# A banded-attention and two-MoE kernel on one core: keys of batch 0 read once, other DMA costs in the planner, and an order picked by a search

## The chip, the cores and the metric

One NeuronCore of a Trainium2 chip runs the whole program. The metric is the device time in microseconds (us) of one execution; the time shown is the median of three. The engines that matter are PE (TensorE: matrix products), DVE (VectorE), ACT (ScalarE), POOL (GpSimd) and SP, whose queue issues every DMA of this kernel. Each engine runs its own instructions strictly in the order in which they were written for it, and waits on semaphores for the others.

## The reference

```python
B, H, S, D = 4, 8, 576, 64            # q, k, v in float32
q_d, k_d, v_d = mean over groups of 4 positions
out_d = softmax(q_d k_d^T / 8) v_d    # "global": 144 x 144 per head
out_up = repeat(out_d, 4)
# "local": keys within 3 positions of the query
scores = where(|i - j| < 4, q k^T / 8, -1e9)
x = out_up + softmax(scores) v        # -> 2304 tokens x 512
h = x @ w_in                          # 512 -> 1024
e = exp(h - max(h)); solu = h * e / (sum(e) + 1e-9)
x = (layernorm(solu) * g_ln) @ w_out  # 1024 -> 512
h = x @ w2_in                         # 512 -> 2048
out = (h * cos(h)) @ w2_out           # 2048 -> 512
```

The four weight matrices arrive in float64. The kernel reads each word pair as integers and builds the float32 value with three DVE operations (`wload`).

## The kernel before, in words

Every product of the two MoE layers is written as three float32r products of a high and a low part (`split` makes the two parts with one ACT and one DVE operation, `mm3` issues the three matmuls). The 2304 tokens go through the first MoE layer in nine groups of 256 (`xsplit`, `h1_half`, `h1_ln`, `ln_t`, `x2`), while the attention is still running; the second layer follows with one plain group of 256 and four groups of 512 by a Strassen-like scheme (`plain_h`, `plain_o`, `quad_h`, `quad_o`).

Attention is made of two kinds of items. A `Glob` (batch b, pair of heads c) does the downsampled attention: `load_qk` reads the whole q and k of two pairs at once (tiles `qt`, `kt`), `load` reads the v of one pair (tile `gv`, 72 partitions), `prep` pools q and k over four positions (DVE, L539) and v (L541, L543), then S, T and V are scores and softmax, transposes, and the product with v. A `Loc` (batch b, third t of the sequence, head group) does the banded attention of 192 queries: its `load` reads a window of q into the block-diagonal tile `diag` (two DMAs on 64 partitions, L594), a window of k (tile `kw`, L596) and windows of v (tile `lv`, L600); S is a mask product on identity weights plus the scores (L606, L608), and V adds the global result and writes `X` (L632). The windows that a `Loc` reads of q and k are the same numbers that `load_qk` reads for the globals.

`X` holds the 2304 tokens (36 blocks of 64). Its still unused tail serves as staging for weights (`stage`, `stage_early`, `stage_dead`, L422 for the load, L427, L429, L431 for the three DVE operations).

The text order of the program is not the order that runs. `arrange` takes all recorded instructions, builds their dependences (`connect`), and list-schedules them: each instruction has an estimated duration (`Step.estimate`), `deadlines` gives it a due time, `forwards` plays the engines and always takes the ready instruction that is due first, `backwards` does the same from the end and gives new due times. Of 2 times 20 plays the order with the earliest estimated end is kept and forced on every engine. A DMA is priced as start + bytes / rate + end, with at most eight in flight. 100 matmuls on the identity (`idle`, L735) need nothing but the mask and are due never, so that they stand on PE wherever the play found nothing else ready; their bank is needed again before the second use of the tag `m`.

Of the kernel before, what the change touches and what calls it, by code (L numbers as in the profile page):

```python
# [1 line left out]

# [18 lines left out]
QB = 64  # L21
# [13 lines left out]
ROUNDS = 20  # L35

# [11 lines left out]
DMA_ISSUE, DMA_START, DMA_END, DMA_RATE, DMA_FLIGHT = 475.0, 1100.0, 935.0, 250.0, 8  # L48
# [50 lines left out]
class Step:  # L99
# [102 lines left out]

def arrange(tc, pools, reopened):
# [9 lines left out]
    def pick(queue, free, ready, rank, last=None):  # L213

        t0, e = min((max(free.get(e, 0.0), min(ready[s] for s in q)), e) for e, q in queue.items() if q)
        q = queue[e]
        s = min((s for s in q if ready[s] <= t0), key=rank)
        if last and e == "PE" and s.mode != last.mode:
            like = [x for x in q if ready[x] <= t0 and x.mode == last.mode and not x.idle]
            if like:  # L220
                x = min(like, key=rank)
                if rank(x)[0] <= rank(s)[0] + PATIENCE:
                    s = x
        q.remove(s)
        return e, s, t0

    def forwards(due, switch):
        left = {s: len(s.preds) for s in steps}
        ready = dict.fromkeys(steps, 0.0)
        queue, free, order, start = {}, {}, {}, {}  # L230
        ticks, last, bus, flying, end = {}, None, 0.0, [], 0.0
        for s in steps:
            if not left[s]:
                queue.setdefault(s.engine, []).append(s)
        for _ in steps:
            e, s, t = pick(queue, free, ready, lambda s: (due[s], s.at), last)
            more = 0.0
            if s.dma:
# [3 lines left out]
                flying.append(bus + DMA_END)  # L242
                more = bus + DMA_END - t - s.ns
                free[e] = t + DMA_ISSUE
            else:
                if e == "PE":
                    t += switch if last and last.mode != s.mode else 0.0
                    last = s
                    if ticks.get(int(t / CLOCK_TICK) - 1, 0.0) < CLOCK_COLUMNS:
                        more = s.ns  # L250
                    i = int((t + s.ns + more) / CLOCK_TICK)
                    ticks[i] = ticks.get(i, 0.0) + s.count
                free[e] = t + s.ns + more
            start[s] = t
            end = max(end, t + s.ns + more)
            order.setdefault(e, []).append(s)
            for b in s.succs:
                ready[b] = max(ready[b], t if b.preds[s] == "begin" else t + after(s, b) + more)
                left[b] -= 1
                if not left[b]:  # L260
                    queue.setdefault(b.engine, []).append(b)
        return start, end, order

    def backwards(start):

        hold = {s: max(DMA_ISSUE, s.bytes / DMA_RATE) if s.dma else s.ns for s in steps}
        late = {s: -(start[s] + s.ns) for s in steps}
        left = {s: len(s.succs) for s in steps}
        ready = dict.fromkeys(steps, 0.0)
        queue, free, begin = {}, {}, {}  # L270
        for s in steps:
            if not left[s]:
                queue.setdefault(s.engine, []).append(s)
        for _ in steps:
            e, s, t = pick(queue, free, ready, lambda s: (-NEVER if s.idle else late[s], -s.at))
            begin[s] = -(t + hold[s])
            free[e] = t + hold[s]
            for a in s.preds:
                ready[a] = max(ready[a], t + hold[s] + after(a, s) - hold[a])
                left[a] -= 1  # L280
                if not left[a]:
                    queue.setdefault(a.engine, []).append(a)
# [818 lines left out]
```

## Time and profile before

| | |
|---|---|
| median of 3 runs | 770.74 us (765.24 to 772.59) |
| the profiled execution, its own time | 774.4 us |
| its span from first to last instruction | 772.6 us |
| busy in it | PE 750.3, DVE 619.1, ACT 448.9, POOL 18.8 us |
| DMA | 106.04 MB, 137 GB/s on the mean |

How to read it: the terms of the prediction are made against the span and the own time of that one execution, 1.8 us apart, and only then carried to the median. A view of windows gives the busy time of each engine in a stretch, so that stretch minus busy is its idle time; PEclk is the granted share of TensorE's clock and "DMA share" the mean busy share of the core's 16 DMA engines. In a timeline, brackets behind a row give the idle time ahead of it and what ended it.

### The profile page before, as it was taken

The page shows a single profiled execution, that of the slowest core. Times are in us where ns is not written, and L with a number is a line of the kernel's source. Part 1 is how long each engine was busy: PE and PEld are TensorE (multiplying, and loading weights), DVE is VectorE, ACT ScalarE, POOL GpSimd, SP SyncE. Part 2 cuts the span into 40 slices and gives each one's busy share as a digit, 9 for nine tenths or more (in the row PEclk, how much of TensorE's full clock was granted, in tenths as well). Part 3 has the DMA queues.
Part 4 walks back from the last instruction along what each step waited for, and adds up shares of the span by engine and source line. Part 5 has one row for each costly group of instructions (what it writes and reads, how often), then busy time and mean ns, then how long its engine had stood idle before and what let it go on. Part 6 is the DMA issues. An engine that isn't in the chain of part 4 may idle for free.

```text
span 772.6 us, 14725 instructions
## 1 busy us (share of the span) xinstructions
PE 750.3 (97%) x5444; PEld 647.4 (84%) x5444; DVE 619.1 (80%) x1379; ACT 448.9 (58%) x1036; POOL 18.8 (2%) x38
## 2 busy tenths in 40 slices
PE   5899999999999999999999999999999999999997
PEld 3566788897888887989988988988898889889896
DVE  5799999999988789776289998777778676887673
ACT  2466776756646455445377766565556665556544
POOL 3000000000000000000000000000000000000000
PEclk9799999999999999999999999999999999999999
DMA  9987865767785657631356433223211331113211
GB/s 237 260 237 197 239 165 176 192 175 223 217 265 145 201 165 229 210 108 39 107 150 178 137 120 99 56 82 110 69 43 54 123 97 44 39 56 108 56 29 54
DMA packets 86520, 106.04 MB, mean 137 GB/s; under 512 B 26384, under 2 KB 59440, under 8 KB 86448
## 3 DMA queue, kind: packets, MB, share of 16 engines
q1 hardware_dynamic: 86448, 105.10, 46.7%
q8 instruction: 43, 0.70, 0.4%
q14 instruction: 29, 0.24, 0.1%
HBM read 87.77 MB, written 17.30 MB: 136 GB/s over the span
## 4 chain that ended last, share of the span: by engine, by line
PE 54%; DVE 29%; DMA 8%; issue 4%; ACT 3%; POOL 1%; SPq 1%; DVEq 0%; POOLq 0%; ACTq 0%
PE s L399 6%; PE s L398 6%; PE s L397 6%; PE oa L397 4%; PE oa L399 3%; PE oa L398 3%; PE ob L397 3%; PE ob L398 3%; PE ob L399 3%; DMA X<-in_w2i_dram 3%; DVE P L390 3%; PE x L398 2%; DVE e L675 2%; DVE sm L491 2%; PE x L399 2%
## 5 line engine op out<-in xcount | busy, mean ns | idle before, releaser
L397 PE MATMUL x<-P,R 128*128 128x256 f32 x288 | 81.2, 284 | 1.5 <-ACT P L389 1.5
L398 PE MATMUL x<-P,R 128*128 128x256 f32 x288 | 81.3, 283 | 0.2 <-DVE P L390 0.2
L399 PE MATMUL x<-P,R 128*128 128x256 f32 x288 | 81.2, 283 | 0.0
L399 PE MATMUL s<-R,S_l 128*128 128x256 f32 x256 | 71.8, 282 | 0.0
L398 PE MATMUL s<-R 128*128 128x256 f32 x256 | 71.5, 280 | 0.0
L397 PE MATMUL s<-R 128*128 128x256 f32 x256 | 71.0, 281 | 0.0
L397 PE MATMUL h<-R,P 128*128 128x512 f32 x144 | 61.1, 424 | 0.5 <-DVE e L675 0.4
L494 ACT ACTIVATE le<-ls,sm 128x70 f32<-128x70 f32 x144 | 44.3, 320 | 26.3 <-DVE sm L492 12.8
L398 PE MATMUL h<-R,P 128*128 128x512 f32 x144 | 58.8, 408 | 0.0
L399 PE MATMUL h<-R,P 128*128 128x512 f32 x144 | 58.5, 406 | 0.0
L397 PEld LDWEIGHTS x<-P,R 128*128 128x128 f32 x288 | 54.0, 188 | 2.8 <-ACT P L389 2.3
L398 PEld LDWEIGHTS x<-P,R 128*128 128x128 f32 x288 | 54.2, 188 | 1.4 <-DVE P L390 1.1
L399 PEld LDWEIGHTS x<-P,R 128*128 128x128 f32 x288 | 54.2, 188 | 1.0 <-issue 0.8
L398 PE MATMUL s<-R,w2i 128*128 128x256 f32 x192 | 54.2, 283 | 0.2 <-DVE R L390 0.2
L399 PE MATMUL s<-R,w2i 128*128 128x256 f32 x192 | 54.0, 282 | 0.0
L397 PE MATMUL s<-R,w2i 128*128 128x256 f32 x192 | 53.8, 282 | 0.0
L389 ACT ACTIVATE GR<-a 128x1024 fp32r<-128x1024 f32 (+1 forms) x40 | 39.1, 977 | 24.3 <-DVE a L895 24.3
L389 ACT ACTIVATE w2i<-wo 128x512 fp32r<-128x512 f32 x58 | 36.2, 624 | 23.5 <-PE ob L399 15.8
L398 PEld LDWEIGHTS s<-R 128*128 128x128 f32 x256 | 48.3, 189 | 0.7
L399 PEld LDWEIGHTS s<-R,S_l 128*128 128x128 f32 x256 | 48.4, 189 | 0.0
L397 PEld LDWEIGHTS s<-R 128*128 128x128 f32 x256 | 47.8, 188 | 0.8
L892 ACT ACTIVATE a<-a 128x1024 f32<-128x1024 f32 (+1 forms) x40 | 38.9, 972 | 15.6 <-DVE a L890 15.5
(164 smaller groups left out, 2195.3 us busy)
## 6 DMA issues: line engine op xcount, KB each, us to landing
wo<-drw SPq DMA_DIRECT2D x80, 256.0 KB
X<-in_w2o_dram SPq DMA_DIRECT2D x32, 256.0 KB
X<-in_w2i_dram SPq DMA_DIRECT2D x32, 256.0 KB
lv<-in_vl_dram SPq DMA_DIRECT2D x48, 105.0 KB
kt<-in_k_dram SPq DMA_DIRECT2D x8, 594.0 KB
kw<-in_k_dram SPq DMA_DIRECT2D x24, 198.0 KB
qt<-in_q_dram SPq DMA_DIRECT2D x8, 576.0 KB
diag<-in_q_dram SPq DMA_DIRECT2D x48, 96.0 KB
```

Of the source, the lines that this page charges most:

```text
L389: nc.scalar.activation(out=hi, in_=src, func=AF.Copy)
L390: nc.vector.tensor_tensor(out=lo, in0=src, in1=hi.bitcast(F32), op=ALU.subtract)
L397: nc.tensor.matmul(ps, lh, rh, start=start, stop=False)
L398: nc.tensor.matmul(ps, lh, rl, start=False, stop=False)
L399: nc.tensor.matmul(ps, ll, rh, start=False, stop=stop)
L491: nc.vector.tensor_reduce(out=neg, in_=src, axis=AX.X, op=ALU.max, negate=True)
L494: nc.scalar.activation(out=e[:, j, :], in_=src[:, j, :], func=AF.Exp, bias=neg[:, j:j + 1], scale=scale, accum_out=ssum[:, j:j + 1])
L675: nc.vector.scalar_tensor_tensor(out=s, in0=p, scalar=GAIN, in1=s, op0=ALU.mult, op1=ALU.mult, accum_out=st[:, 2 + i:3 + i])
L892: nc.scalar.activation(out=a, in_=a, func=AF.Sin, scale=0.5)
```

## The change

Four things are changed.

1. For batch 0, `kt` no longer lies in the `qk` buffers but in `X` (ten of the blocks from block 9 on, which batch 1 fills later). A `Loc` of batch 0 takes its keys from there instead of reading `kw` again (6 loads fewer). For the first two thirds of batch 0 the block-diagonal `diag` is filled by ACT from `qt` (8 copies) instead of by DMA (8 loads fewer). Both `load_qk` of batch 0 stand first in the text.
2. `gv` is read in two DMAs of 64 and 8 partitions instead of one of 72 (16 loads more).
3. The planner's DMA price: the rate is 235 instead of 250 bytes per ns, bytes count 1.5 times where the contiguous run is under 512 bytes, and a DMA on fewer than 128 partitions with over 128 columns lands 2,000 ns later.
4. After the 40 plays, 78 fixed random draws are applied to the best due times, each shifting the due times of some (tile, engine) groups within some stretch of time; the result is played once and kept if its estimated end is earlier. `forwards`, `backwards` and `deadlines` are rewritten with heaps and lists over instruction numbers; apart from `land` and `bytes` they price what they did.

```diff
-DMA_ISSUE, DMA_START, DMA_END, DMA_RATE, DMA_FLIGHT = 475.0, 1100.0, 935.0, 250.0, 8
+DMA_ISSUE, DMA_START, DMA_END, DMA_RATE, DMA_FLIGHT = 475.0, 1100.0, 935.0, 235.0, 8
+DMA_RUN, DMA_SHORT, DMA_PART = 512, 1.5, 2000.0
+SEARCHED = 1.0
+DRAWS = (80000010, 80000013, 80000019, 80000027, 80000037, 80000077, 80000279, 80000333, 80000445, 80000518,
...
@@ Step.estimate
         if self.dma:
             self.bytes = n * list(out.ap)[0][1] * width(out)
-            return DMA_START + self.bytes / DMA_RATE + DMA_END
+            if list(out.ap)[-1][1] * width(out) < DMA_RUN:
+                self.bytes *= DMA_SHORT
+            self.land = DMA_END + (DMA_PART if list(out.ap)[0][1] < 128 and n > 128 else 0.0)
+            return DMA_START + self.bytes / DMA_RATE + self.land
...
+def draws(seed):
+    s = (seed * 2862933555777941757 + 3037000493) % 2 ** 62
+    for i in range(4):
+        s = (s * 6364136223846793005 + 1442695040888963407) % 2 ** 62
+    while True:
+        s = (s * 6364136223846793005 + 1442695040888963407) % 2 ** 62
+        yield s >> 31
...
@@ arrange, behind the 40 plays
+    names = [s.outs[0].bass_ap.tensor.name + s.engine for s in steps]
+    rank = {g: i for i, g in enumerate(sorted(set(names)))}
+    known = [d for d in chosen if abs(d) < NEVER / 2]
+    lo, hi = min(known), max(known)
+    due = chosen
+    for seed in DRAWS:
+        r = draws(seed)
+        at = lo + (hi - lo) * SEARCHED * (next(r) % 100000 / 100000.0)
+        wide = (10e3, 30e3, 100e3, 300e3, 2 * (hi - lo))[next(r) % 5]
+        size = (100.0, 300.0, 1000.0, 3000.0, 6000.0)[next(r) % 5]
+        share = (3, 10, 30, 100)[next(r) % 4]
+        shift = []
+        for _ in rank:
+            u = next(r) % 100
+            x = (next(r) % 2001 - 1000) / 500.0 * size
+            shift.append(x if u < share else 0.0)
+        due = [d + shift[rank[g]] if at - wide / 2 <= d < at + wide / 2 else d for d, g in zip(due, names)]
+    start, end, order = forwards(due, MODE_SWITCH)
+    if end < best:
+        best, kept, chosen = end, order, due
...
@@ Glob.load_qk
-                QK[self.b, self.c // 2] = [att.tile([128, NT3, 2, QT + 2 * HALO], F32, tag="qk", name=n, bufs=3)[:, :, :, :w]
-                                           for n, w in (("qt", QT), ("kt", QT + 2 * HALO))]
+                d = QK[self.b, self.c // 2] = []
+                for n, w in (("qt", QT), ("kt", QT + 2 * HALO)):
+                    if self.b == 0 and n == "kt":
+                        x = X[:, S // QB + 5 * (self.c // 2):][:, :5].rearrange("p b k q -> p (b k q)")
+                        d.append(x[:, :NT3 * 2 * w].rearrange("p (t h s) -> p t h s", t=NT3, h=2))
+                    else:
+                        d.append(att.tile([128, NT3, 2, QT + 2 * HALO], F32, tag="qk", name=n, bufs=3)[:, :, :, :w])
@@ Glob.load
-            nc.sync.dma_start(out=self.v, in_=vg[self.b, self.c])
+            for r in (slice(0, 64), slice(64, SH)):
+                nc.sync.dma_start(out=self.v[r], in_=vg[self.b, self.c, r])
@@ Loc.load
-                kt = att.tile([128, 2, QT + 2 * HALO], F32, tag="k", name="kw", bufs=2)
                 for j in range(2):
                     r = slice(64 * j, 64 * j + 64)
-                    nc.sync.dma_start(out=diag[i][r, :, :, j, :],
-                                      in_=q[self.b, self.cc, r, self.t].rearrange("p h (a s) -> p h a s", a=NB))
-                nc.sync.dma_start(out=kt, in_=k[self.b, self.cc, :, self.t])
+                    if self.b == 0 and self.t < 2:
+                        nc.scalar.copy(out=diag[i][r, :, :, j, :],
+                                       in_=QK[0, self.cc][0][r, self.t].rearrange("p h (a s) -> p h a s", a=NB))
+                    else:
+                        nc.sync.dma_start(out=diag[i][r, :, :, j, :],
+                                          in_=q[self.b, self.cc, r, self.t].rearrange("p h (a s) -> p h a s", a=NB))
+                if self.b == 0:
+                    kt = QK[0, self.cc][1][:, self.t]
+                else:
+                    kt = att.tile([128, 2, QT + 2 * HALO], F32, tag="k", name="kw", bufs=2)
+                    nc.sync.dma_start(out=kt, in_=k[self.b, self.cc, :, self.t])
@@ ahead of the main loop
-    for g in globs(0, 0):
-        g.load_qk()
+    for cc in range(NPP):
+        for g in globs(0, cc):
+            g.load_qk()
```

What the new prices and the draws do to the order is seen only in the instructions as they stand on each engine. Three places follow. Line numbers of the changed kernel are higher; the names are the same, except that the keys of batch 0 are now called `X`.

SP at the start of the program, before (`qt`, `kt`: whole q and k of two pairs; `kw`, `diag`: their windows; `lv`, `gv`: v):

```order
L523 DMA qt<-in_q_dram 128x6x192
L523 DMA kt<-in_k_dram 128x1188
L596 DMA kw<-in_k_dram 128x396
L594 DMA diag_116<-in_q_dram 64x6x64 x2
L596 DMA kw<-in_k_dram 128x396
L523 DMA qt<-in_q_dram 128x6x192
L529 DMA gv<-in_vg_dram 72x1024 x2
L594 DMA diag_115<-in_q_dram 64x6x64 x2
L523 DMA kt<-in_k_dram 128x1188
L422 DMA X<-in_w1i_dram 128x512
L600 DMA lv<-in_vl_dram 70x384 x4
L596 DMA kw<-in_k_dram 128x396
```

And the same place in the change:

```order
L609 DMA qt<-in_q_dram 128x6x192
L609 DMA X<-in_k_dram 128x1188
L609 DMA qt<-in_q_dram 128x6x192
L609 DMA X<-in_k_dram 128x1188
L616 DMA gv<-in_vg_dram 64x1024
L616 DMA gv<-in_vg_dram 8x1024
L616 DMA gv<-in_vg_dram 64x1024
L616 DMA gv<-in_vg_dram 8x1024
L694 DMA lv<-in_vl_dram 70x384 x4
L503 DMA X<-in_w1i_dram 128x512 x3
L616 DMA gv<-in_vg_dram 64x1024
L616 DMA gv<-in_vg_dram 8x1024
```

The second q and k now stand right behind the first, the windows of q and k are gone, and three loads of the first weight (`w1i`) stand ahead of the third v instead of one.

ACT at its start, before (`le` and `ge` are the exponentials of local and global scores, `at` the transposed ones):

```order
L494 ACT_TABLE_LOAD
L494 ACTIVATE le,sm<-ls,sm 128x70 x6
L494 ACTIVATE ge,sm<-gs,sm 128x144
L618 COPY at<-lt 70x384
L494 ACTIVATE ge,sm<-gs,sm 128x144
```

And in the change:

```order
L681 ACT_TABLE_LOAD
L681 COPY diag_116<-qt 64x6x64 x2
L575 ACTIVATE le,sm<-ls,sm 128x70 x3
L681 COPY diag_115<-qt 64x6x64 x2
L681 COPY diag_116<-qt 64x6x64
L575 ACTIVATE le,sm<-ls,sm 128x70 x3
L575 ACTIVATE ge,sm<-gs,sm 128x144
L681 COPY diag_116<-qt 64x6x64
L712 COPY at<-lt 70x384
```

The table load and the first copies now stand ahead of the first exponential and need only the first `qt`.

DVE ahead of the twelfth `h1` maximum, before (`m<-h` is that reduction; `X<-X` rows build staged weights; rows 374 to 385 of DVE):

```order
L427 TENSOR_SCALAR X<-X 128x256
L429 SCALAR_TENSOR_TENSOR X<-X 128x256 x2
L431 SCALAR_TENSOR_TENSOR X<-X 128x256
L496 TENSOR_SCALAR sm<-sm 128x3
L431 SCALAR_TENSOR_TENSOR X<-X 128x256
L497 RECIPROCAL sm<-sm 128x3
L539 TENSOR_REDUCE pooled_113<-kt 128x288
L491 TENSOR_REDUCE sm<-gs 128x3
L498 TENSOR_TENSOR ge<-ge,sm 128x432
L492 TENSOR_SCALAR sm<-sm 128x3
L491 TENSOR_REDUCE sm<-ls 128x3
L660 TENSOR_REDUCE m<-h_2258 128x1
```

And in the change (rows 364 to 373):

```order
L626 TENSOR_REDUCE pooled_113<-kt 128x288
L578 RECIPROCAL sm<-sm 128x3
L628 TENSOR_TENSOR gv<-gv 72x2x256
L579 TENSOR_TENSOR le<-le,sm 128x210
L754 TENSOR_REDUCE m<-h_2203 128x1
L779 SCALAR_TENSOR_TENSOR st<-st 128x1
L630 TENSOR_TENSOR gvs<-gv 72x256
L508 TENSOR_SCALAR X<-X 128x256
L628 TENSOR_TENSOR gv<-gv 72x2x256
L754 TENSOR_REDUCE m<-h_2256 128x1
```

Counted over the whole stretch from the start, 394 DVE instructions stand ahead of this reduction before and 381 now; among them are 6 scalar_tensor_tensor and 2 tensor_scalar operations on staged weights fewer.

## Rows read from the trace of the kernel before

**Rows 1.** The page: busy time, and granted clock and DMA in 40 slices.

```profile
PE 750.3 (97%) x5444; PEld 647.4 (84%) x5444; DVE 619.1 (80%) x1379; ACT 448.9 (58%) x1036; POOL 18.8 (2%) x38
...
PEclk9799999999999999999999999999999999999999
DMA  9987865767785657631356433223211331113211
```

**Rows 2.** Windows by stage: us, PE, PEld, DVE, ACT, POOL busy, PEclk, DMA share, GB/s.

```profile
0.00:60.00 60.00, 49.70 (x412) 32.98 (x413) 43.74 (x132) 26.91 (x111) 5.85 (x20) 0.91 0.94 247
60.00:160.00 100.00, 99.40 (x876) 80.01 (x875) 99.40 (x302) 71.63 (x257) 3.27 (x5) 1.00 0.67 187
160.00:340.00 180.00, 174.37 (x1452) 151.48 (x1451) 158.24 (x499) 95.76 (x311) 8.55 (x11) 1.00 0.66 199
340.00:480.00 140.00, 138.40 (x940) 126.49 (x939) 106.01 (x177) 84.81 (x136) 1.10 (x2) 1.00 0.40 121
480.00:760.00 280.00, 279.78 (x1738) 249.79 (x1737) 210.47 (x272) 167.27 (x220) 0.00 (x0) 1.00 0.23 67
```

**Rows 3.** The fill matmuls alone (tile idle): us, PE busy, PEclk, DMA share, GB/s.

```profile
0.00:40.00 40.00, 13.87 (x59) 0.88 0.96 250
40.00:80.00 40.00, 8.27 (x42) 1.00 0.82 224
```

**Rows 4.** Timeline of DVE, first 31 us and the twelfth maximum: start, us.

```profile
5.27 1.35 DVE L539 TENSOR_REDUCE pooled<-qt 128x288 f32<-128x1152 f32 x1 [4.36 <-DMA qt<-in_q_dram]
...
10.65 0.38 DVE L491 TENSOR_REDUCE sm<-ls 128x3 f32<-128x210 f32 x1 [2.43 <-PE ls L608]
...
12.76 1.35 DVE L539 TENSOR_REDUCE pooled<-qt 128x288 f32<-128x1152 f32 x1 [1.07 <-DMA qt<-in_q_dram]
...
29.80 0.69 DVE L541 TENSOR_TENSOR gv<-gv 72x512 f32<-72x512 f32 x1 [2.19 <-DMA gv<-in_vg_dram]
...
153.00 0.68 DVE L660 TENSOR_REDUCE m<-h 128x1 f32<-128x512 f32 x1
```

**Rows 5.** DMA issues of the page: line, KB each.

```profile
kw<-in_k_dram SPq DMA_DIRECT2D x24, 198.0 KB
...
diag<-in_q_dram SPq DMA_DIRECT2D x48, 96.0 KB
```

**Rows 6.** Timeline of ACT at its start: the table load and a copy of 384 columns.

```profile
11.31 1.28 ACT L494 ACT_TABLE_LOAD   x1 [11.31 <-DVE sm L492]
...
16.84 0.47 ACT L618 COPY at<-lt 70x384 f32<-70x384 f32 x1 [1.06 <-PE lt L616]
```

**Rows 7.** Timeline of PE: start, us, line.

```profile
6.90 3.09 PE L735 MATMUL idle<-mask,identb 128*128 128x350 bf16 x11 [1.29 <-POOL mask L730]
9.83 1.45 PE L608 MATMUL ls<-kw,diag 128*128 128x70 f32 x12
...
30.76 0.43 PE L564 MATMUL gt<-ident,ge 128*72 128x128 f32 x1 [2.26 <-DVE ge L498]
...
39.86 0.72 PE L397 MATMUL h<-R,P 128*128 128x512 f32 x1
...
89.53 0.40 PE L397 MATMUL h<-R,P 128*128 128x512 f32 x1
89.76 0.40 PE L398 MATMUL h<-R,P 128*128 128x512 f32 x1
90.09 0.92 PE L629 MATMUL lv<-at,lv 70*64 70x64 f32 x24
```

**Rows 8.** DVE groups by shape, staged weights: count, busy us, mean ns, idle before.

```profile
L431 DVE SCALAR_TENSOR_TENSOR X<-X 128x256 int32<-128x256 int32 x64 | 26.6, 419 | 0.5
...
L427 DVE TENSOR_SCALAR X<-X 128x256 int32<-128x256 int32 x64 | 18.1, 288 | 11.3 <-DMA X<-in_w2i_dram 6.6 <-DMA X<-in_w2o_dram 2.4 <-DMA drw<-X 1.8
```

**Rows 9.** Timeline of SP: one load of v.

```profile
20.87 0.30 SPq L529 DMA_DIRECT2D gv<-in_vg_dram  x1
```

**Rows 10.** Windows: the one in which the granted clock fell, columns as in rows 2.

```profile
20.00:40.00 20.00, 17.74 (x161) 10.91 (x158) 14.58 (x49) 9.20 (x40) 0.00 (x0) 0.75 1.01 264
```

More of the change, by code (lines that the diff above doesn't have):

```diff
@@ L227, in forwards @@
-    def forwards(due, switch):
-        left = {s: len(s.preds) for s in steps}
-        ready = dict.fromkeys(steps, 0.0)
-        queue, free, order, start = {}, {}, {}, {}
-        ticks, last, bus, flying, end = {}, None, 0.0, [], 0.0
[L232 to L237, printed above, removed]
+    n = len(steps)
@@ new lines, in forwards @@
+    def forwards(due, switch):
+        left, ready = npreds[:], [0.0] * n
+        coming = [[] for _ in engines]
+        there = [{} for _ in engines]
+        free, soonest = [0.0] * len(engines), [NEVER] * len(engines)
+        order, start = [[] for _ in engines], [0.0] * n
+        ticks, last, bus, flying, end = {}, None, 0.0, [], 0.0
+        for i in range(n):
+            if not left[i]:
+                heappush(coming[home[i]], (0.0, i))
+                soonest[home[i]] = 0.0
+        for _ in range(n):
+            t = min(soonest)
+            e = soonest.index(t)
+            new, old = coming[e], there[e]
+            while new and new[0][0] <= t:
+                i = heappop(new)[1]
+                kind = None if idle[i] else modes[i]
+                if kind in old:
+                    heappush(old[kind], (due[i], i))
+                else:
+                    old[kind] = [(due[i], i)]
+            heap = min(old.values()) if len(old) > 1 else next(iter(old.values()))
+            if last and e == pe and last in old and old[last][0][0] <= heap[0][0] + PATIENCE:
+                heap = old[last]
+            i = heappop(heap)[1]
+            if not heap:
+                del old[None if idle[i] else modes[i]]
+            s, more = steps[i], 0.0
@@ L249, in forwards @@
                     if ticks.get(int(t / CLOCK_TICK) - 1, 0.0) < CLOCK_COLUMNS:
[L250 to L258, printed above, removed]
+                        more = ns[i]
@@ new lines, in forwards @@
+                    k = int((t + ns[i] + more) / CLOCK_TICK)
+                    ticks[k] = ticks.get(k, 0.0) + s.count
+                free[e] = t + ns[i] + more
+            soonest[e] = free[e] if old else max(free[e], new[0][0]) if new else NEVER
+            start[i] = t
+            if t + ns[i] + more > end:
+                end = t + ns[i] + more
+            order[e].append(i)
+            for b, begin, lag in succs[i]:
+                r = t if begin else t + lag + more
+                if r > ready[b]:
+                    ready[b] = r
@@ L259, in forwards @@
                 left[b] -= 1
                 if not left[b]:
[L261 removed]
+                    h = home[b]
+                    r = ready[b]
+                    heappush(coming[h], (r, b))
+                    if r < free[h]:
+                        r = free[h]
+                    if r < soonest[h]:
+                        soonest[h] = r
         return start, end, order
     def backwards(start):
[L266 removed]
@@ L267, in backwards @@
[L267 to L279, printed above, removed]
+        late = [-NEVER if idle[i] else -(start[i] + ns[i]) for i in range(n)]
@@ L300, in arrange @@
+    soon, first, t = [0.0] * n, {}, 0.0
+    for i, s in enumerate(steps):
+        soon[i] = max([0.0] + [soon[a] + lag for a, lag in preds[i]])
+        if home[i] == pe and not idle[i]:
+            soon[i] = first[i] = t = max(t, soon[i])
+            t += ns[i]
     best = NEVER
     for _ in range(ROUNDS):
-        due = deadlines(pe)
+        due = deadlines(first)
         for turn in range(2):
```

83 lines of the change are left out of this document (49 added, 34 removed), and 7 rows, old and new, of the table DRAWS.

## The prediction

> **What bounds the kernel now.** I read the page first. PE is busy 97% of the span, so at first sight no edit of loads can matter [rows 1]. The windows by stage say where that is not so. From 480 us on PE is busy 279.8 of 280 us: nothing is to be had there. From 60 to 160 us PE and DVE are both busy 99.4 of 100 us. In the first 60 us, however, PE idles 10.3 us and DVE 16.3 us, while the DMA engines are busy 94% of the time at 247 GB/s [rows 2]. PE's 49.7 busy us there are flattered too: 13.9 us of the first 40 and 8.3 us of the next 40 are fill matmuls that compute nothing [rows 3], and between 20 and 40 us the mean granted clock is 0.75, which means 1.2 instead of 2.4 GHz for half of the window; in it PE waited 2.26 us, until 30.76 us [rows 10, 7].
>
> So the start is short of data, and what it loses is carried on: DVE, which catches up on nothing between 60 and 160 us, hands its delay to every later step. The reader should see in these rows that DVE's idle time of the first 60 us, not PE's busy share, is the quantity to follow. Its large pieces are: 4.36 us until the first q, 2.43 us until the first local scores, 1.07 us until the second q, 2.19 us until the fourth v [rows 4]. With 0.9 us ahead of the first wait that is 11.0 us; the other 5.3 us are short waits on PE and ACT.
>
> **The change part by part.**
>
> *Loads removed.* 6 `kw` of 198 KB and 8 `diag` of 96 KB [rows 5] are 1,956 KB, 2.0 MB. At 247 GB/s [rows 2] this is 8.1 us of a DMA phase that is full. Adding up the sizes of SP's rows in order, 12.0 MB had been asked for when the last `w1i` load was issued, and 10.0 MB now. The second q stands behind 1.2 MB instead of 1.8, so its 1.07 us of wait goes. The fourth v stands behind more bytes than before, 5.8 MB against 5.3, because four `w1i` loads now stand ahead of it instead of one; but its load was issued only at 20.87 us [rows 9], behind windows of q and k that are gone. I leave 0.5 of its 2.19 us.
>
> *Copies added.* 8 ACT copies of 64 x 384 at 0.47 us [rows 6] are 3.8 us on an engine that idles 33.1 of the first 60 us [rows 2]. They cost nothing there, except that two stand ahead of the first exponential: first q at 5.3 us, table load 1.28 us, two copies 0.94 us, so `diag` is ready at 7.5 us. The table load stood on the chain at 11.31 us [rows 6] and leaves it. On PE six fills stand ahead of the first scores instead of eleven; eleven took 2.93 us at the start [rows 7], so six take 1.6 us. POOL now makes the identity late, at the latest when its last mask was done before, 6.9 us [rows 7]; the first scores then run at 8.5 to 9 us instead of 9.83. DVE's wait of 2.43 us becomes about 1.6.
>
> *v in two pieces.* 16 more issues of 0.30 us [rows 9] are 4.8 us of SP, against 14 issues that are gone: nothing. Whether 64 + 8 partitions land sooner than 72, no row shows; I take zero, with 1 us either way for the four v of batch 0.
>
> *DVE idle of the first 60 us, summed.* Start 5.3 (unchanged), first scores 1.6, second q 0, fourth v 0.5, short waits 3.1 instead of 5.3, because three weight loads' worth of DVE work (12 operations) now stands between the softmaxes and fills their gaps. That is 10.5 us instead of 16.3: 5.8 us sooner. If none of the short waits goes and the first scores come no sooner, it is 13.5 (2.8 sooner); if nearly all go, 7.3 (9 sooner).
>
> *Order moved.* By the order, 394 DVE instructions stood ahead of the twelfth `h1` maximum, which ran at 153.0 us [rows 4], and 381 now. Among those gone are 6 at 0.419 and 2 at 0.288 us [rows 8], 3.1 us; softmax pieces and two more v steps nearly cancel. DVE is full in that stretch, so I count 2.8 us. Ahead of the seventeenth maximum 16 staging operations fewer stand; there PE binds, and I count no more. PE has the room: until 153 us it idled 10.9 us, and its 22.1 us of fills could be 14 (eleven at the low clock took 2.93, half of that for the rest); with a start at 6.9 us that leaves 12 us.
>
> *Tile shapes.* By the order PE changes between full tiles and tiles of 64 rows or columns 124 times instead of 149. One change costs 0.10 us: matmuls of 512 columns start 0.23 us apart, and 0.33 apart where the next is a 64-column one [rows 7]. 25 of them are 2.5 us; where DVE binds they are worth nothing, so I take 1 us (ends 0 and 2.5).
>
> *Later stages.* From 160 to 340 us PE idles 5.6 us [rows 2], and DVE waits 10.8 us for DMAs ahead of staged weights [rows 8]. The new prices leave loads more time, but the draws were kept by an estimate and not by a clock. I take no change, with 5 us better and 4 us worse as ends. From 340 us on PE has 1.8 us to lose until 760 us.
>
> *Sum.* 5.8 + 2.8 + 1 = 9.6 us. The profiled execution took 774.4 us of its own time, span 772.6; it becomes 764.8. That run lies 3.7 us above the median of 770.7, so the forecast for the median is 761.
>
> **A rule that speaks against a part.** The fourth v's load was issued in 0.30 us, and its landing ended a DVE wait of 2.19 us [rows 9, 4]. The Trainium skill, "DMA: Bandwidth & Descriptors", section "Anatomy of one DMA", says that every DMA carries a fixed cost of about 2 us whatever its size. By it the split of v would add, if pieces queue up behind each other, an estimated 8 us for the four v of batch 0 and eat most of the gain; if they fly side by side, nothing. No row of before separates the two, which is why the split has a rival of its own below.
>
> **The rivals.**
>
> *The gain is given back.* The start is 6 us sooner, but between 160 and 340 us DVE waits longer for staged loads and PE for DVE, since PE idles only 5.6 us there and DVE 21.8: a chain of latencies, not a load, sets the pace. For it: 10.8 us of DMA waits ahead of the first staging operation [rows 8], and DMA is still 66% busy. Against it: fewer staging operations stand early. Half of the 9.6 us would stay: 766.
>
> *More than forecast.* The new DMA prices also take out the waits of 160 to 340 us: 5 of PE's 5.6 us, and the tile changes count in full, 1.5 more. 761 - 6.5 = 754. For it: the waits named are all on DMAs that the old price took for faster. Against it: the same staging ring, the same loads.
>
> *The pieces of v land late.* Four v of batch 0 at 2 us more each, from the wait of 2.19 us taken as the price of one late v: 8 us of the gain gone, 769. For it: SP now issues four loads for two v. Against it: the pieces are issued 0.3 us apart.
>
> *Slower: fills at the low clock.* 86 fills instead of 59 stand ahead of PE's first `h1` matmul, which ran at 39.86 us [rows 7] and in the forecast runs about then, and PE takes them in order. At 0.27 us each, as the first eleven took, they are 23 us, at half of that 11.5. With 13.6 us of real work at the full rate (the order's rows up to there by the starts of such rows) and a start at 6.9 us this is 32 us at the high clock, and nothing is lost; at the low one throughout it is 57 us, 17 late, and DVE, which has the maxima of `h1` to take, waits for it: 761 + 17 = 778. It turns slower than before from 10 us late on, when the low clock holds for 0.7 of that stretch; at half of it, as in [rows 10], it costs 5 us of the gain. For it: the clock has fallen once already, around a wait. Against it: runs of fills keep PE busy where it waited. The Trainium skill, "TensorE: Matmul & The Clock Gate", Part 1, says that the low state is the default and that only a busy PE releases it; the 0.75 of [rows 10] agrees, and by that rule the fills themselves speak against this rival.
>
> That the draws do nothing, since they are kept only if the estimate falls, is out: without them the same code gives an order that differs in 963 of DVE's 1,345 places.
>
> **How the numbers follow.** Forecast 0.52 (own range 757 to 765), more 0.15, given back 0.19, v late 0.05, slower 0.09. A difference of 1% (7.7 us) is about what a measurement of this kernel can tell. Under 763.0 lie 0.47 of the forecast and all of "more": 0.62. Over 778.4 lies most of the last rival with its worse ends: 0.07. The rest, 0.31, is within 1%. The range reaches from 751, "more" with the start's upper end (9 instead of 5.8), to 772, "given back" with the start's lower end (2.8) and part of the 4 us that the later stages may lose.
>
> **What would show it.** Right: DVE idle of about 10 us instead of 16.3 in the first 60 us; the twelfth maximum at about 144 us; no fall of the granted clock between 12 and 45 us that lasts; the first local scores before 9.5 us; PE idle of 160 to 340 us still 4 to 6 us; from 480 us on a busy PE again. Wrong at the start: the third or fourth v, or a `w1i` load, ending waits of DVE of over 2 us together. Wrong later: the twelfth maximum early, but PE idle of more than 10 us between 160 and 480 us. Wrong altogether: a first `h1` matmul after 45 us.

## The result and the profile after

The changed kernel takes 760.69 us (median of 4; 757.74 to 763.05), the kernel before beside it 769.78: the ratio is 0.988, 95% interval 0.984 to 0.992. Run once more, beside three of the experiments, it took 759.06 us (median of 6), ratio 0.987 (0.984 to 0.990). The forecast was 761.0, and "faster by over 1%" had the largest chance. The profiled execution took 760.38 us, its span is 758.6 us.

The page after, with the rows that answer to [rows 1]:

```profile
PE 745.1 (98%) x5444; PEld 646.8 (85%) x5444; DVE 616.7 (81%) x1379; ACT 452.7 (60%) x1044; POOL 18.7 (2%) x38
...
PEclk9999999999999999999999999999999999999999
DMA  8877866575776476464263542123122331122201
```

The windows by stage after (us; busy time of PE, PEld, DVE, ACT, POOL; PEclk, DMA share, GB/s), to be laid beside [rows 2]:

```profile
0.00:60.00 60.00, 53.14 (x466) 37.09 (x467) 50.48 (x152) 34.95 (x137) 5.84 (x20) 1.00 0.79 225
60.00:160.00 100.00, 99.62 (x893) 84.08 (x893) 99.87 (x302) 71.04 (x260) 5.30 (x6) 1.00 0.72 191
160.00:340.00 180.00, 179.22 (x1475) 155.93 (x1473) 154.70 (x489) 96.40 (x302) 6.43 (x10) 1.00 0.65 197
340.00:480.00 140.00, 139.28 (x935) 126.50 (x935) 111.08 (x179) 88.88 (x136) 1.15 (x2) 1.00 0.40 118
480.00:746.00 266.00, 265.46 (x1647) 236.76 (x1646) 199.74 (x261) 159.04 (x210) 0.00 (x0) 1.00 0.23 69
```

DVE idles 9.5 us in the first 60 instead of 16.3, and does 6.7 us more work there. DVE is full from 60 to 160 us as before. What I had not expected stands in the third row: from 160 to 340 us PE idles 0.8 us instead of 5.6. The end is a busy PE again.

Four rows of DVE's timeline after answer to [rows 4]:

```profile
5.45 1.35 DVE L626 TENSOR_REDUCE pooled<-qt 128x288 f32<-128x1152 f32 x1 [4.53 <-DMA qt<-in_q_dram]
...
10.07 0.38 DVE L572 TENSOR_REDUCE sm<-ls 128x3 f32<-128x210 f32 x1 [1.74 <-PE ls L702]
...
19.19 0.38 DVE L572 TENSOR_REDUCE sm<-ls 128x3 f32<-128x210 f32 x1 [1.14 <-PE ls L702]
...
142.28 0.68 DVE L754 TENSOR_REDUCE m<-h 128x1 f32<-128x512 f32 x1
```

All waits of DVE in the first 60 us after, by what ended them (us in total, times, longest):

```profile
DVE pooled L626 <- DMA qt<-in_q_dram: 4.5, 1, 4.5
DVE sm L572 <- PE ls L702: 3.3, 3, 1.7
DVE pooled L814 <- PEq L1180: 0.8, 1, 0.8
DVE sm L577 <- ACT le L575: 0.2, 1, 0.2
DVE pooled L626 <- DMA X<-in_k_dram: 0.2, 1, 0.2
```

The waits for the second q and for v are gone altogether; local scores are waited for. The twelfth maximum runs 10.7 us sooner (153.00 before). All 36 maxima of the tile `m`, before and then after (min/median/max ns, first and last start in us):

```profile
L660 DVE TENSOR_REDUCE m<-h x36: 656/684/693, 54.4 to 357.9; 128x1 f32<-128x512 f32 x36
```

```profile
L754 DVE TENSOR_REDUCE m<-h x36: 657/683/693, 54.7 to 344.0; 128x1 f32<-128x512 f32 x36
```

The first is no sooner, the last 13.9 us. So of the 14.0 us between the two spans 10.7 lie ahead of the twelfth maximum, 3.2 between it and the last, and 0.1 behind the last. PE's timeline after, at its start ([rows 7]):

```profile
8.65 2.67 PE L702 MATMUL ls<-X,diag 128*128 128x70 f32 x12
...
17.45 0.42 PE L651 MATMUL gt<-ident,ge 128*72 128x128 f32 x1
...
18.99 0.27 PE L651 MATMUL gt<-ident,ge 128*72 128x128 f32 x1
...
39.38 0.49 PE L478 MATMUL h<-R,P 128*128 128x512 f32 x1
```

The twelve score products take 2.67 us where they took 1.45, and the same transposition 0.42 us at 17.45 and 0.27 at 18.99: up to about 18.9 us PE runs at 1.2 GHz. The column PEclk reads 1.00 there, so at a start it is no evidence; the durations are. The fills went up in the first 40 us as the order said, 86 against 59 [rows 3], and nearly vanished behind them:

```profile
0.00:40.00 40.00, 18.02 (x86) 1.00 0.88 255
40.00:80.00 40.00, 2.17 (x9) 1.00 0.76 205
```

The group of staged weights [rows 8] waits 9.2 us instead of 11.3:

```profile
L508 DVE TENSOR_SCALAR X<-X 128x256 int32<-128x256 int32 x64 | 18.3, 286 | 9.2 <-DMA dra<-X 5.4 <-DMA drw<-X 2.1 <-DMA X<-in_w2o_dram 1.6
```

### The profile page after: what moved, and what is told of

It reads as the page before. It is cut to its first block, busy times and chain, and to the rows that moved or that the text cites. A ratio compares the mean times of both kernels' runs of the same rounds, so it can differ in the third digit from the quotient of the medians.

```text
span 758.6 us, 14716 instructions
## 1 busy us (share of the span) xinstructions
PE 745.1 (98%) x5444; PEld 646.8 (85%) x5444; DVE 616.7 (81%) x1379; ACT 452.7 (60%) x1044; POOL 18.7 (2%) x38
## 4 chain that ended last, share of the span: by engine, by line
PE 81%; DVE 12%; DMA 3%; ACT 2%; issue 1%; POOL 1%; SPq 0%; POOLq 0%; DVEq 0%; ACTq 0%
PE s L478 7%; PE s L480 7%; PE s L479 7%; PE oa L478 4%; PE ob L478 4%; PE ob L480 4%; PE oa L480 4%; PE oa L479 4%; PE ob L479 4%; PE h L478 3%; PE x L478 3%; PE x L479 3%; PE ls L702 3%; PE x L480 3%; PE h L480 3%; PE h L479 3%
## 5 line engine op out<-in xcount | busy, mean ns | idle before, releaser
L478 PE MATMUL x<-P,R 128*128 128x256 f32 x288 | 80.2, 286 | 0.3 <-ACT P L470 0.3
L479 PE MATMUL x<-P,R 128*128 128x256 f32 x288 | 79.1, 282 | 0.3 <-DVE P L471 0.3
L480 PE MATMUL x<-P,R 128*128 128x256 f32 x288 | 78.9, 282 | 0.0
L478 PE MATMUL s<-R 128*128 128x256 f32 x256 | 70.3, 282 | 0.1
L479 PE MATMUL s<-R 128*128 128x256 f32 x256 | 70.4, 281 | 0.0
L478 PEld LDWEIGHTS x<-P,R 128*128 128x128 f32 x288 | 53.5, 188 | 1.6 <-ACT P L470 0.7
L479 PEld LDWEIGHTS x<-P,R 128*128 128x128 f32 x288 | 53.3, 188 | 1.5 <-DVE P L471 0.6
L480 PEld LDWEIGHTS x<-P,R 128*128 128x128 f32 x288 | 53.2, 188 | 0.3
L478 PE MATMUL s<-R,w2i 128*128 128x256 f32 x192 | 52.3, 282 | 0.2 <-DVE wr L1094 0.2
L480 PE MATMUL s<-R,w2i 128*128 128x256 f32 x192 | 52.5, 282 | 0.0
L479 PE MATMUL s<-R,w2i 128*128 128x256 f32 x192 | 52.1, 281 | 0.0
L471 DVE TENSOR_TENSOR GR<-a,GR 128x1024 fp32r<-128x1024 f32 (+1 forms) x40 | 44.6, 1114 | 7.7 <-ACT GR L470 7.6
```

The costliest lines, as they stand in the source:

```text
L471: nc.vector.tensor_tensor(out=lo, in0=src, in1=hi.bitcast(F32), op=ALU.subtract)
L478: nc.tensor.matmul(ps, lh, rh, start=start, stop=False)
L479: nc.tensor.matmul(ps, lh, rl, start=False, stop=False)
L480: nc.tensor.matmul(ps, ll, rh, start=False, stop=stop)
```

## The experiments

Two kinds follow, and they don't say the same. In the first, a part of the change is undone and the planner finds a new order for all engines. In the second, the changed kernel's order is pinned, and only what the diff shows is added or moved. All ratios are to the kernel before, run on the same chip; 0.01 is 7.7 us.

### Parts undone or alone, with a new order each

**No draws.**

```diff
-DRAWS = (80000010, 80000013, 80000019, 80000027,
...
+DRAWS = ()
```

> The change with its draws left out: same loads, same new DMA prices, the order is the best of the 40 plays. Theory A (the data of the first 60 us make the gain): DVE idles at most 11.5 us of the first 60 us, and two thirds of the 9 us are kept: about 764 us. Theory B (the searched order makes it): the start is as early, but PE idles 5 us or more between 160 and 340 us again, and DVE's staging stands ahead of the maxima as in the kernel before; at least 767 us.

763.71 us, ratio 0.994 (0.991 to 0.996). Its windows, where they differ from those of the changed kernel:

```profile
60.00:160.00 100.00, 97.87 (x860) 80.20 (x859) 99.25 (x300) 69.65 (x251) 4.24 (x6) 1.00 0.68 189
...
340.00:480.00 140.00, 137.50 (x930) 125.37 (x929) 111.58 (x184) 87.82 (x135) 1.10 (x2) 1.00 0.41 125
```

PE idles 2.1 us from 60 to 160 and 2.5 from 340 to 480 us (0.4 and 0.7 with the draws), with its largest wait, 1.6 us, for an ACT operand of the second layer. The twelfth maximum runs at 144.7 us instead of 142.3.

**The change itself again**, to lay beside it.

> The changed kernel itself once more, beside the three others on one chip, so that they can be told from it and not from a run of another day. Both theories of the draws expect about 760.5 us; the ratio to before stands at 0.988 so far and at 0.994 without draws, with intervals that touch. If the ratio comes out at 0.991 or under, the draws are worth at least 2 us; at 0.994 they are worth nothing that can be measured.

Ratio 0.987 (0.984 to 0.990): the interval does not touch that of the kernel without draws. So the order with the draws is 0.5 to 0.7% faster than the one without (by the two measurements of the change), 4 to 5 us: about half of the whole gain. It is one searched order against one that was not searched, and orders found anew for nearly the same program scatter from 0.994 to 0.999 below, so that the search as such finds better orders is not shown.

Nor are the draws what took out PE's idle time of 160 to 340 us: without them it is 0.3 us, with them 0.8. The profile without draws is best laid beside this run's, since in both PE's clock rises at about 10 us (rows of this run's start stand under *Fills sooner*). The twelfth maximum then moves from 144.7 to 140.3 us, the last from 344.3 to 341.5, the end of the span from 760.6 to 755.4: what the searched order gains lies ahead of the twelfth maximum and behind the last, and 1.6 us are given back between them.

**No draws, the old DMA price.**

```diff
+DRAWS = ()
...
-DMA_ISSUE, DMA_START, DMA_END, DMA_RATE, DMA_FLIGHT = 475.0, 1100.0, 935.0, 235.0, 8
-DMA_RUN, DMA_SHORT, DMA_PART = 512, 1.5, 2000.0
+DMA_ISSUE, DMA_START, DMA_END, DMA_RATE, DMA_FLIGHT = 475.0, 1100.0, 935.0, 250.0, 8
+DMA_RUN, DMA_SHORT, DMA_PART = 512, 1.0, 0.0
```

> The loads of the change alone: no draws, and the old DMA prices (rate 250, no extra for short runs or few partitions). Theory A: as without draws, 764 to 765 us. Theory C (the prices make the order of loads that brings the first 60 us): DVE idle of the first 60 us is back at 13 us or more, and the time is 768 us or more.

764.95 us, ratio 0.995 (0.993 to 0.997). From 160 to 340 us PE idles 3.1 us:

```profile
160.00:340.00 180.00, 176.95 (x1444) 153.99 (x1443) 153.04 (x479) 94.64 (x295) 7.31 (x10) 0.99 0.65 196
```

The same window has 0.3 us of idle time without draws and with the new price. But kernels with one and the same order (below) show 0.3 to 2.5 us there, and the two ratios' intervals overlap: the new price is worth 1 us or nothing. The twelfth maximum runs at 142.7 us here, as early as in the first profile with the draws.

**No draws, the loads put back** (`kw`, `diag` and `kt` read as before; the new price and the split v stay).

```diff
-                    if self.b == 0 and n == "kt":
+                    if False and n == "kt":
...
-                    if self.b == 0 and self.t < 2:
+                    if False:
...
-                if self.b == 0:
+                if False:
...
-    for cc in range(NPP):
-        for g in globs(0, cc):
-            g.load_qk()
+    for g in globs(0, 0):
+        g.load_qk()
```

> New prices and the split of v, without draws, but q and k windows of batch 0 read again as before (kw and diag by DMA, kt in its old buffer). Theory A: no gain, 768 to 772 us, DVE idle of the first 60 us at 14 us or more. Theory C: 764 to 766 us, since the prices alone put the loads in a better order.

767.81 us, ratio 0.998 (0.996 to 1.000). DVE idles 14.3 us in the first 60. DVE's timeline and then PE's:

```profile
11.67 1.35 DVE L627 TENSOR_REDUCE pooled<-qt 128x288 f32<-128x1152 f32 x1 [3.49 <-DMA qt<-in_q_dram]
...
14.93 0.38 DVE L573 TENSOR_REDUCE sm<-ls 128x3 f32<-128x210 f32 x1 [1.91 <-PE ls L703]
```

```profile
7.02 7.25 PE L830 MATMUL idle<-mask,identb 128*128 128x350 bf16 x30 [0.62 <-POOL mask L825]
14.11 1.45 PE L703 MATMUL ls<-kw,diag 128*128 128x70 f32 x12
```

The wait for the second q is back, 3.49 us. But this is no clean undoing. The new price calls `diag` (64 partitions, short runs) late by 2 us and more, and the planner put 30 fills ahead of the first scores where the kernel before had eleven and ran them at 9.83 us [rows 7]; PE ended the fills and only then took them up. So the late start may be as much the price's work as that of the loads; no run separates the two.

**The loads alone**, on the kernel before: old price, v in one piece, no draws.

> Only the first part of the change, on the kernel before: keys of batch 0 read once, diag filled by ACT; v in one piece, old DMA price, no draws. Theory A (the loads carry the start's gain whatever else is changed): DVE idle of the first 60 us about 9 us instead of 16.3, the twelfth maximum 5 us or more before 153 us, time 764 to 767. Rival B (the order is found anew for each edit, and its waits further on decide): DVE idle at the start is down as well, but the gain is not to be seen at the thirty-sixth maximum (357.9 us before), because a new wait of 2 us or more stands between 160 and 340 us; time 768 to 771.

764.61 us, ratio 0.994 (0.992 to 0.996). DVE idles 10.0 us in the first 60 and the twelfth maximum runs at 144.7 us. The last of the 36 runs at 348.5 us, 9.4 sooner than before, although a wait stands on the way. Its windows and that wait on PE:

```profile
0.00:60.00 60.00, 53.40 (x464) 37.84 (x465) 50.01 (x152) 35.04 (x137) 5.89 (x20) 1.00 0.87 247
...
160.00:340.00 180.00, 175.61 (x1458) 153.93 (x1457) 152.14 (x477) 95.26 (x303) 8.79 (x11) 1.00 0.63 192
```

```profile
171.04 0.52 PE L710 MATMUL lt<-ident,le 128*70 128x128 f32 x3 [2.79 <-DVE X L726]
```

So this part by itself gives some 4 us (4.1 between the medians, 4.5 by the ratio), by what A said of the start and with the wait that B foresaw. With price and split added and no draws it is 0.9937: those two add nothing that can be measured.

**No draws, v in one piece** (loads and new price kept).

```diff
-            for r in (slice(0, 64), slice(64, SH)):
-                nc.sync.dma_start(out=self.v[r], in_=vg[self.b, self.c, r])
+            nc.sync.dma_start(out=self.v, in_=vg[self.b, self.c])
```

> As without draws, but v in one DMA of 72 partitions again (the order is planned anew). Forecast's term: no difference beyond 1 us from the kernel without draws. Rival (the split is what brings v sooner): DVE waits for the third or fourth v for 2 us again and the time is 2 to 3 us longer than without draws. Rival of the prediction (the pieces land late): 2 us or more shorter.

767.84 us, ratio 0.999 (0.997 to 1.001): some 4 us lost, but not at the start, where DVE idles 9.3 us and waits for no v. It goes further on. The waits, of DVE and of PE:

```profile
167.96 0.29 DVE L509 TENSOR_SCALAR X<-X 128x256 int32<-128x256 int32 x1 [3.82 <-DMA lv<-in_vl_dram]
```

```profile
169.20 0.85 PE L710 MATMUL lt<-ident,le 128*70 128x128 f32 x3 [1.78 <-DVE X L726]
```

A staging operation stands ahead of what PE needs and waits for a load. Behind the wait PE's granted clock falls, which the windows show (column PEclk, third from the end):

```profile
165.00:170.00 5.00, 3.22 (x41) 2.71 (x40) 2.04 (x8) 0.33 (x1) 0.00 (x0) 0.83 0.95 310
170.00:175.00 5.00, 5.00 (x15) 3.60 (x13) 2.81 (x12) 2.65 (x14) 0.00 (x0) 0.50 0.82 233
```

So the wait costs more than its own length: from 170 to 175 us PE is busy at 1.2 GHz. The forecast of no difference beyond 1 us missed, but neither rival's mechanism was at work. Since the loads alone, also with v in one piece, gave 0.994, the loss is most likely that of this order and not of the single DMA; no run with the order pinned tests it.

### One thing added or moved, the order pinned

**40 more DVE operations** of 128 x 128, one after every fourth DVE instruction, from place 190 on (in the stretch in which DVE is full) or from place 1030 on (where PE binds).

```diff
+    at = {190 + 4 * i: x for i, x in enumerate(extra)}
...
+    for i in range(40):
+        nc.vector.tensor_scalar(out=spare, in0=ident, scalar1=1.0, scalar2=None, op0=ALU.mult)
```

> The change with every instruction in its place, and 40 spare DVE operations of 128 columns (about 5 us together; they only write a scratch tile) put one after every fourth DVE instruction between about 60 and 120 us. Theory A (DVE sets the pace there): the whole of their busy time appears, about 5 us more than the change, 766 us. Rival (PE sets the pace there, being busy as much as DVE): at most 1 us more.

> The same 40 spare DVE operations put one after every fourth DVE instruction in the second layer, from about 480 us on, where PE is busy all the time and DVE idles a quarter. Theory A: within 1 us of the change, 761 us. If DVE sat on the path there too: up to 5 us more.

From place 190, where they ran from 73.7 to 134.3 us: 765.56 us, ratio 0.993 (0.990 to 0.996), the twelfth maximum at 147.1 us, 4.8 later. From place 1030, where they ran from 436.5 to 581.6 us: 762.72 us, 0.990 (0.986 to 0.993), the twelfth at 141.8 us and the last at 344.4. The window of the first with its twelfth maximum, and the maxima of the second:

```profile
60.00:160.00 100.00, 96.67 (x850) 79.13 (x849) 99.94 (x328) 67.89 (x243) 5.43 (x6) 1.00 0.69 180
```

```profile
147.10 0.68 DVE L766 TENSOR_REDUCE m<-h 128x1 f32<-128x512 f32 x1
```

```profile
L766 DVE TENSOR_REDUCE m<-h x36: 658/682/693, 54.2 to 344.4; 128x1 f32<-128x512 f32 x36
```

In the first it is as theory A had it: DVE stays full and PE starves by 3.3 us. In that stretch a DVE microsecond is about a microsecond of the end. Later it is less than half of one, and not none: of a span of 761.2 us 416.8 lie behind the last maximum, where the profiles of the same order without these operations there have 413.4 to 414.6, or 415.1 with them placed early. So some 2 us of the 5 appear, 0.8 of them a wait of PE for DVE; by the ratios the times are 1 to 3 us apart, and the intervals overlap. The first of the two is the step on which the whole sum rested.

**2.0 MB of loads more at the start**, ten of 192 KB with runs of 1,536 bytes, DRAM to DRAM; and then **eight of 96 KB with runs of 256 bytes**.

```diff
+    at = (2, 2, 4, 4, 4, 12, 15, 18, 20, 20)
...
+    for i in range(10):
+        nc.sync.dma_start(out=again[i], in_=q[1 + i // 4, i // 2 % 2, :, i % 2].rearrange("p h s -> p (h s)")[:, :384])
```

> The change with every instruction in its place, and 10 extra loads of 192 KB (1.97 MB together, from DRAM to a DRAM scratch that nothing reads) put on SP among the first 20 loads, as many bytes as the removed windows had. Theory A (the full DMA phase is what the change relieves): DVE idle of the first 60 us rises from 9.5 towards 15 us and the time by 4 to 7 us, 765 to 768 us. Rival (not the bytes but which loads stand first): at most 2 us more.

> The changed kernel with its order kept and eight more loads of 96 KB in runs of 256 bytes (what diag had), DRAM to DRAM: two ahead of the second q, two ahead of the first v, two ahead of the third v, two behind the fourth. 0.8 MB more, against 2.0 MB in runs of 1,536 bytes that cost nothing. Theory A (short runs hold the DMA engines, so it was the kind of the loads and not their bytes): the second q and the v land late, DVE idle of the first 60 us goes from 9.5 to 12 us or more, the twelfth maximum from 142.3 to 144 us or later, time 763 or more. Theory B (what the change took away was that the first scores waited for their own windows behind the whole q and k, a matter of place in the queue): idle 9 to 10 us, twelfth maximum 142 to 143 us, time 760 to 761.

759.98 us, ratio 0.986 (0.983 to 0.990), and 758.33 us, 0.987 (0.984 to 0.990). Neither costs anything. The first window of each:

```profile
0.00:60.00 60.00, 53.13 (x467) 37.08 (x468) 50.56 (x152) 35.02 (x137) 5.84 (x20) 1.00 0.87 258
```

```profile
0.00:60.00 60.00, 53.14 (x470) 37.12 (x471) 50.85 (x153) 35.22 (x137) 5.84 (x20) 1.00 0.84 239
```

The rate rises from 225 to 258 GB/s, and DVE's idle time stays at 9.4 and 9.2 us. So bytes were not what the changed kernel's start lacked. Theory A falls in both. The kernel without draws and with the old price points the same way; its first window shows the DMA engines 99% busy, and DVE idles 9.0 us:

```profile
0.00:60.00 60.00, 53.36 (x477) 37.71 (x477) 50.98 (x157) 37.09 (x142) 5.92 (x20) 1.00 0.99 252
```

Three limits: the kernel before, with its engines 94% busy, was given no more bytes; only two of the added loads stand ahead of the second q, 0.4 and 0.2 MB, where the kernel before had 0.6 MB more than the changed one; and no run wrote added short runs into SBUF.

**Thin fills:** each fill is 70 columns wide instead of 350, its price kept so that the order stays.

```diff
-        nc.tensor.matmul(idle[:, :(NB + 2) * WIN], identb, mask.rearrange("p j s -> p (j s)"), start=True, stop=True)
+        nc.tensor.matmul(idle[:, :WIN], identb, mask.rearrange("p j s -> p (j s)")[:, ::5], start=True, stop=True)
```

> The change with every instruction in its place, but the 100 fill matmuls have 70 columns instead of 350 (the planner still counts them as 350 wide). The chain of waits of the change runs through the fills for a quarter of the first 60 us. Reading 1 (fills stand in PE's queue ahead of real work and delay it): 2 to 5 us less, 756 to 759 us. Reading 2 (DVE's work sets the start, the fills only fill): within 1 us while the clock stays up. Rival of the prediction (the clock falls without them): the granted clock of the first 45 us drops and the time is 3 us or more longer.

769.6 us, ratio 0.997 (0.994 to 1.000); DVE idles 17.6 us in the first 60, and the twelfth maximum runs at 151.4. PE's timeline says why:

```profile
57.01 0.77 PE L480 MATMUL h<-R,P 128*128 128x512 f32 x1
57.71 0.55 PE L663 MATMUL gv<-at,gvs 72*64 72x96 f32 x8
...
59.52 0.40 PE L479 MATMUL h<-R,P 128*128 128x512 f32 x1
```

One `h1` matmul takes 0.77 us at 57.01 and 0.40 at 59.52: the low level lasted until about 57.7 us. Fills that compute nothing carry 9 us at the twelfth maximum, and 7 to 8 us of the result by the ratios.

**Fills sooner:** POOL makes what the fills need first, and four fills more stand ahead of the first scores, so that PE begins at 4.58 us.

```diff
+MOVED = 4
...
+            for i, n in enumerate(("identb", "mask", "diag", "ident")):
...
+        moved = fills[runs[0]:][:MOVED]
...
+        rest = rest[:2] + front + rest[2:]
```

> The changed kernel with two orders altered: POOL makes the identity of the fills and the whole mask first, ahead of diag and ident, and four fills from a later run stand with the first six on PE. Nothing is added or left out. Theory A (the granted clock stays low until 18.9 us because PE starts at 6.57 us and then waits often; DVE's two waits for local scores, 1.74 and 1.14 us, come of that): PE starts at about 5 us, the clock is high by 9 us, the first scores' reduction runs near 9 us instead of 10.07, DVE idle of the first 60 us 7 to 8 us instead of 9.5, the twelfth maximum 1.5 to 2.5 us sooner than 142.3 and the end too: 758 to 759.5 us. Rival B (four more fills ahead only stand in the way, and the clock falls again): first reduction at 10 us or later, idle 9.5 or more, 761 or more.

759.88 us, ratio 0.988 (0.985 to 0.991): no gain. A window and PE's timeline:

```profile
5.00:20.00 15.00, 14.91 (x65) 10.17 (x63) 11.31 (x32) 10.15 (x35) 2.01 (x6) 1.00 0.95 268
```

```profile
5.17 3.07 PE L855 MATMUL idle<-mask,identb 128*128 128x350 bf16 x10
8.04 2.67 PE L728 MATMUL ls<-X,diag 128*128 128x70 f32 x12
...
18.45 0.42 PE L677 MATMUL gt<-ident,ge 128*72 128x128 f32 x1
...
21.16 0.30 PE L677 MATMUL gt<-ident,ge 128*72 128x128 f32 x1
```

PE begins 2 us sooner, is busy 14.91 of 15 us, and stays at 1.2 GHz until about 20.4 us all the same. The first reduction did run at 9.47 us, but what it won was lost to a wait of 1.02 us for k and to slow scores: DVE idles 9.9 us. My theory A fell, and not for the reason that B gave.

The unchanged kernel's second profile shows the other side. PE's timeline there:

```profile
8.65 2.22 PE L702 MATMUL ls<-X,diag 128*128 128x70 f32 x12
...
15.95 0.28 PE L651 MATMUL gt<-ident,ge 128*72 128x128 f32 x1
```

The same program has its high clock from about 10.2 us on. DVE then idles 7.9 us in the first 60, and the 36 maxima lie some 2 us sooner:

```profile
L754 DVE TENSOR_REDUCE m<-h x36: 655/682/692, 52.7 to 341.5; 128x1 f32<-128x512 f32 x36
```

The Trainium skill, "TensorE: Matmul & The Clock Gate", Part 1, says that the number of slow matmuls at a start differs from run to run of one kernel. The trace agrees: 18.9 against 10.2 us, and the spans are 758.6 and 755.4.

## Why the prediction was right, and where it was not

*The quantity to follow* was the right one: 40 DVE operations cost 4.8 us at the twelfth maximum, and the same 40 later some 2 us.

*Loads removed.* "8.1 us of a DMA phase that is full" was the wrong reason. 2.0 MB added to the changed kernel cost nothing, so bytes were not what the start lacked. The loads alone nevertheless give some 4 us. What changed with them is which loads come first: the second q and k directly behind the first, three loads of `w1i` early. DVE then had work at hand, and its waits for q (1.07) and v (2.19) fell to nothing. That it is the order of arrival and not the load on the DMA engines is shown only as far as the two pinned runs go.

*Copies, start of the scores.* Forecast 8.5 to 9 us, measured 8.65. But they ran at 1.2 GHz, and DVE's wait was 1.74 us, where I had 1.6.

*DVE idle of the start.* Forecast 10.5 us (5.8 sooner), measured 9.5, and 7.9 in the second profile. The difference lies in the short waits, of which more went than I took, and in the clock of the start.

*v in two pieces.* Taken at zero; no wait for v is left, and none with v in one piece either. The rival of late pieces is out, since DVE waits for none of them. The Trainium skill's "DMA: Bandwidth & Descriptors", section "Anatomy of one DMA", gives its fixed cost of about 2 us for DMAs issued from GpSimd, while SP issues these loads; the estimated 8 us that the prediction worked out from it do not show here, and whether the pieces queued up no row tells.

*Order moved, tile shapes.* Start and order together were to bring the twelfth maximum 8.6 us forward, to about 144 us. It came at 142.3 and 140.3 us; the orders without draws put it at 144.7 (loads alone, and all but the draws), 144.9 (v in one piece) and 142.7 (old price). So the draws may be at work in this term as well, but one order without them came as early as the first profile of the change. The 1 us taken for tile shapes no run tells apart. (By the prediction's own rows PE's fills at half their length come to 14.9 us, not 14; nothing hangs on it.)

*Later stages* is the step that failed: "the draws were kept by an estimate and not by a clock. I take no change", with PE's idle time "still 4 to 6". It is 0.8 us, and the stretch from the twelfth to the last maximum shrank by 3.2 us, where the sum had nothing for it. The reason given failed with it: the draws, kept by an estimate, go with 4 to 5 us, half of the gain. But those are two things. The idle time of this stretch is gone without the draws too (0.3 us), and it is 2.4 to 4.4 us in the four other orders found anew; what decides it between such orders stays open.

*Why the sum is right nonetheless.* The profiled executions lie 14.0 us apart and the medians 9.1. I took the extra 3.7 us of the execution before as if they stood outside my terms. They probably stand inside the first: its granted clock was low for half of the window from 20 to 40 us [rows 10], and ten microseconds at half the clock are up to 5 us. No second profile of the kernel before was taken, so where the time went is argued and not shown. That the time goes with the clock is on record: of the 71 executions of the kernel before beside the experiments, the 26 with a mean granted clock of 0.999 or 1.000 have a median of 767.3 us, the nine at 0.995 or less 773.6; the profiled one had 0.992. The ten of the changed kernel all have 0.999 or 1.000, so a small part of its gain is likely a clock that falls no more. Taken so, the start is over-counted for the median by about what the later stages were under-counted, and that the two errors are of one size is luck.

*More than forecast.* Its waits did go, 4.8 of the 5 us, but not its price: it had 754. Of the 4.8 us 3.2 reached the last maximum, and the new price is not shown to be the cause, as two other orders with it have 2.4 and 3.1 us of idle time there.

*Slower: fills at the low clock.* It did not come, but a low clock is dear: with thin fills it held until 57.7 us, and that cost 9 us at the twelfth maximum. The clock can also stay low while fills run: it rose at 18.9 us in the first profile, with PE busy from 6.57 us on without a break, and at 20.4 in the kernel with PE busy 14.91 of 15 us. "Runs of fills keep PE busy", which I held against the rival, was therefore a weak reason. What saved the forecast is that some 9 us more at the low level went with only 2 to 3 us, which fits a start at DVE's pace and not PE's; no run tests that for the first 60 us.

*Given back.* Out for the change: its waits of 160 to 340 us went away. For single parts it is true; the loads alone and v in one piece each met a new wait of 1.8 to 2.8 us on PE at 169 to 171 us.

## What to carry to other kernels

Where a planner sets the order, undoing one edit measures the edit and a new order together, and such orders scattered here by some 4 us; pin the order and add or move one thing to price a mechanism. Follow the engine that is full behind a gap, and test that it binds by giving it idle work at two places. Do not call a stage short of bandwidth because the DMA engines are over 90% busy: add bytes and look.

## What the hardware showed that was not expected

- The time at which PE's clock first goes up is not fixed by the program: 10.2 and 18.9 us in two executions of the same kernel, 20.4 in one whose PE was busy from 4.58 us on. A first profile of a start is uncertain by about that: 1.6 us of DVE idle time and 3.2 us of span here.
- The column PEclk shows 1.00 in these stretches at the start; only durations at two places (0.42 and 0.27 us for one transposition) tell.
- DMA engines that are 79% busy at 225 GB/s took 1.97 MB more at 258 GB/s, and DVE waited no longer for it.
- The clock can fall behind a short wait or not: with v in one piece it read 0.50 from 170 to 175 us, after a PE wait of 1.78 us; with the loads alone it read 1.00 from 165 to 180 us, with a wait of 2.79 us in it.
